# One kernel, two orders: the same attention and mixer operations of a Trainium2 core put into a new sequence

## The chip, the core and the metric

The kernel runs on one core of a Trainium2 chip. A core has five engines that run their own instruction streams side by side: TensorE (PE in the profile; its weight loads are shown apart, as PEld), VectorE (DVE), ScalarE (ACT), GpSimd (POOL) and SyncE (SP). They work on SBUF, the core's memory of 128 partitions, and on PSUM, eight banks into which PE writes. Each engine takes its instructions strictly in the order in which the program holds them; where one needs the result of another engine it waits on a semaphore, and everything behind it on its engine waits too. DMA transfers are issued from POOL and SP (and can be from ACT).

The metric is the time of one execution in microseconds. Three timed runs of the kernel before gave 284.23, 285.07 and 284.23 us; the median is 284.23.

## The reference

Eight sequences (B = 8) of 576 positions go through an attention of 8 heads of 64, and the result, 576 x 512 per sequence, through an MLP mixer:

```
attention:  scores = q k^T / 8, position i sees block j of 64 when i // 64 >= j // 64
            x = softmax(scores) v                    heads side by side: x is 576 x 512
token mix:  u = x + ( relu(x^T w_tok1) w_tok2 )^T    w_tok1 576 x 256, w_tok2 256 x 576
channels:   out = u + relu(u w_ch1) w_ch2            w_ch1 512 x 1536, w_ch2 1536 x 512
```

Inputs and output are float32; the matrix products run in bfloat16 with float32 sums.

## The kernel before, in words

The kernel is one Python function that first describes about 1,500 operations and then emits them. `P.add(engines, cost, emit, deps, ...)` appends an operation: the engines that may run it, what it depends on, which PSUM banks it takes and gives back, and the function that emits its instructions. Operations are numbered in the order of these calls. Nothing is scheduled while the kernel is built: `Plan.placed` reads the string `ORDER`, a list of words such as `627Tbd`. The number is the operation, the capital letter its engine (T for PE, A for ACT, D for DVE, P for POOL, S for SP) and the small letters are the PSUM banks that it takes (a to d are the banks `mm`, e to h the banks `late`, s and t two double banks `sc` that exist only during the first attention). The operations are emitted in the order of the words, so that the words of one engine are that engine's queue. The semaphores follow from what the operations read and write.

The stages, with the operations that the text speaks of:

- **Start.** DVE clears some tiles (`init_tiles`, L340); one of them, 9, zeroes the operand of the warming matmuls. `raise_clock` has PE run 11 matmuls of 512 columns on zeros (operation 43, L366) and then single extra ones (44 to 80, L373) wherever ORDER places them; their results are used by nobody.
- **Loads.** K and Q of a batch come in two groups of four heads. For the first group of batch 0, SP loads K in two halves (16, 13), ACT casts them to bfloat16 (17, 14; L395), and POOL loads Q in three pieces (21, 19, 23). All other loads of K, Q and V, and of the weights, are issued by POOL (L419, L471, L482, L505) and change the type on the way. DVE then transposes K and Q in blocks of 32 x 32 (L442).
- **Attention.** `score_set` (L569) multiplies 32 rows of K by Q for four heads at a time, which use the four 32-row strips of the PE array side by side, and adds a bar for the masked block. ACT takes the exponential (L587 and L737 in batch 0, L776 after it). The last 64 columns are copied and cleared by DVE or POOL (`tail`, L595 and L600). `head_out` (L617) and `ends_out` (L670, 64 columns of the array) multiply with V, whose extra column of ones gives the sum, and DVE divides (L637, L643, L692, L698).
- **Token mix.** `token_up` (L811, L815), then products with `w_tok2` (L910, in batch 0 L846), to which DVE adds x (L925): that is U. The channel products need U transposed. For batches 0 and 1 PE does it with the identity matrix (operation 12 makes it, on POOL); from batch 2 on SP does it with two DMA transposes per batch (L977), the first two of which are operations 607 and 606.
- **Channel mix.** Batch 0 plainly (`channel_up` L1038, `first_down` L1460). Batches 1 to 3 and the joined last 64 positions of all batches use Strassen-like sums of seven products (`channel_up_half` L1111, `channel_down_fast` L1369), batches 4 to 7 in pairs (`channel_up_fast` L1235). DVE and ACT keep, join and clip the parts (L395, L797, L1150, L1165, L1351), DVE adds the residual (L1393), and SP, at the end also ACT, stores the output (L1435).

Batches overlap: while PE does the channel products of one batch, it also does the attention of the next ones. ORDER is where that interleaving is written down. The line numbers are those of the profile of the kernel before; in the changed file the lines behind ORDER are one less.

Of the kernel before, what the change touches and what calls it, by code (L numbers as in the profile page):

```python
# [27 lines left out]
class Plan:  # L28
# [69 lines left out]
    16S 0A 11D 10D 13S 9D 21P 1D 2D 43Ta 5D 19P 4D 3D 23P 33P 27P 14A 25P 31P 15D 29P 17A 20D 37P 44Tb 45Tb 46Tb 22D  # L98
    47Ta 36P 48Ta 49Ta 18D 50Ta 51Ta 52Ta 35P 53Ta 24D 54Ta 55Ta 56Ta 125Ts 34P 100Ttbc 179P 126A 28D 57Ta 58Ta 59Ta
    176P 60Ta 61Ta 26D 62Ta 101A 12P 106Ts 63Ta 32D 182P 64Ta 107A 65Ta 104Tt 42P 30D 66Ta 67Ta 105A 68Ta 39P 123Ts  # L100
    102D 103D 69Ta 70Ta 41P 119A 71Ta 157Tt 124A 112Td 40P 113T 116Ta 108Tb 114D 120A 38P 109T 115D 138Ts 158A 181D
    81P 72Td 73Tc 74Tc 121D 75Tc 122D 139A 82P 76Tc 7D 144Tt 110D 111D 84P 135Td 178D 127Tc 145A 161Ts 185P 136D
    117D 137D 140D 131Tb 180D 83P 128T 162A 142Tt 177D 90P 132T 129D 143A 77Td 89P 163Ts 130D 133D 86P 134D 78Td
    164A 118D 141D 159D 200Tdcba 160D 85P 203A 173Te 154Tf 165Tg 202A 91P 174D 166T 155D 156D 201A 184D 92P 205Tbhfc
    204A 183D 169Td 88P 170T 209A 167D 263Ta 168D 208A 175D 150Tc 171D 261Tg 172D 207A 187D 267Td 206A 87P 186D
    146Te 262A 147T 264A 151T 268D 237Tgbfh 152D 339P 6D 148D 269Ta 153D 241A 149D 273Td 189P 240A 270D 281Tc 239A
    274D 265Te 190P 238A 271Ta 8D 282D 275Tb 266A 191P 193Tdhfg 276A 272D 283Te 196A 277Tc 342P 194A 315Ta 278D
    306Tb 197A 188P 294Td 195A 279Tc 284A 192P 318Tf 198D 280D 291Tg 319T 348P 316T 309Tc 317A 310T 257D 93P 320A
    307T 295T 94P 308A 292T 311A 258D 225Teahf 345P 296A 300Tb 227A 95P 285Tc 228A 286T 293D 226A 303Td 287D 229A
    304T 351P 232Tahge 341D 199D 312Tc 230D 233A 305D 313T 234A 231D 288Tf 344D 314A 297Ta 340D 236A 289T 343D 235A  # L110
    210Td 513P 245Tc 290A 211D 213Th 516P 212D 242Te 246D 216Tg 354P 247D 301T 214D 215D 248Td 243D 302A 298T 244D
    355P 217D 219Tc 249D 299A 250D 222Th 220D 254Te 221D 363Tdbaf 255D 256D 251Tc 349D 364A 330Te 352P 252D 365A
    218D 253D 321Td 367A 223D 224D 366A 259D 353P 368Tcghb 420Ta 372A 370A 422Tb 347D 371A 525P 346D 322T 421D 423A
    260D 369A 356Tafgh 323T 359A 357A 350D 424Tb 360A 324D 331T 358A 425D 388Tcadg 361P 514D 430Tb 391A 434Th 332T
    389A 431D 435A 518D 426Td 392A 517D 400Thcbf 390A 515D 428Tg 404A 393P 362D 334Ta 522P 403A 429D 677P 401A 335T
    333D 402A 528P 427D 376Tb 373Tc 394D 527P 96D 395Tdfgh 379Te 526P 377D 396A 374D 336T 375D 397A 519P 378D 380D
    405Tc 398A 680P 381D 382Tb 399A 406D 385Td 407D 432Te 337D 417Tc 383D 386D 433A 530Tafgh 387D 384D 418D 436Td
    419D 531A 440Tb 97D 414Tc 534A 325Te 533A 98D 326T 532A 415D 437A 416D 542Tahgf 99D 441A 438Tc 545A 327T 439D
    544A 444D 463Tgd 543A 445D 448Thb 328D 466A 464Tc 451D 546A 329S 411Ta 408Te 465A 446D 469T 412D 690P 413D 449Tf
    523D 470A 454T 529P 450A 409D 442Ta 410D 452Tc 455A 443D 691P 467Tg 520D 453A 537Taefh 447D 692P 468A 456T 521D  # L120
    538A 473T 689P 524D 539A 471T 679D 540A 683P 596Ta 457D 541A 474D 562Tcefh 597A 678D 458T 566A 681D 594Ta 565A
# [6 lines left out]
    694Tcgab 508D 856P 618T 698A 849D 509T 697A 846D 696A 619D 695A 760Tb 609D 610D 699P 510D 738Tacgh 761A 848D  # L128
    631Tf 742A 611D 942P 628Tb 741A 632D 758Th 700P 740A 853P 629D 739A 845D 635T 759A 726Tcbag 636D 723Th 730A 637T
    724D 729A 725D 717Tf 638D 762Th 727A 764Ta 728A 718D 719D 640T 763D 731P 733Tfcbg 641A 732P 765D 768Th 737A 851D  # L130
    766Td 772S 735A 720Ta 769D 711Tg 736A 746Tc 721D 722D 734A 616Th 767D 714Ta 617A 613Tb 712D 773S 713D 642Tdf
    747D 614A 748D 620T 715D 645A 716D 743Tg 622T 621D 639A 648T 744D 511S 745D 646Tb 854D 512S 649A 861Tcagh 338S
    647A 623D 643Td 863A 624D 652T 862A 644D 752Ta 865A 650T 653D 625T 864A 753D 749Tc 754D 626A 655T 866P 852D
    868Tadhg 867P 651D 656A 755Te 871A 770Tf 775D 952P 869A 654D 794Tbh 756D 750D 872A 751D 951P 795Ta 776D 797A
    779Tgc 757D 939P 796D 870A 780Te 782A 800T 657D 798Ta 781A 855D 783Td 771A 785T 799A 784D 948P 809Tef 801A 953P
    802T 777D 812A 778D 787T 803D 945P 786A 804T 815T 788D 789T 805D 816A 905Tbadg 790D 813Te 908A 807T 906A 814D
    792T 808A 810Td 658D 907A 817T 909A 811D 661Tbh 793A 818D 873Tadcg 662D 819T 875A 943D 667T 876A 820D 877A 944D
    874A 822T 941D 893Tdceg 821D 823A 887Ta 659D 897A 884Tf 663T 894A 888D 889D 895A 885D 886D 896A 940D 900Tadcg
    898P 664D 890Tf 904A 899P 881Te 949D 1037P 903A 925Tb 882D 955P 883D 902A 891D 892D 901A 878Te 947D 1040P
    968Tfcdg 926A 950D 954P 922Ta 969A 879D 665Tb 880D 1046P 971A 946D 970A 923D 924D 1043P 972A 956Tedfa 666D 913Tc  # L140
    668D 959A 916Tg 914D 669T 958A 915D 917D 957A 918D 660D 960A 910Td 919Tc 961D 995Tgafe 911D 1052P 920D 921D 670D
    999A 927Tc 1053P 998A 912D 962D 997A 791D 1050P 963Tdbef 996A 671T 928A 1042D 967A 1041D 966A 1000Tacgf 965A
    672D 979Te 964A 1039D 976Tb 1003A 673T 980D 977D 1004A 981D 978D 1002A 988Tbedg 1001A 674D 973Tc 991A 1047D
    1022Tf 676S 990A 974D 975D 989A 1038D 982Ta 992A 985Tc 806D 1054Tdbhe 983D 1023A 984D 993P 1020Tg 1044D 994P
    1055A 1051P 1048D 1058A 1045D 931Ta 1057A 1008Td 986D 1056A 987D 933Tf 932D 1021A 929Tc 1009D 934D 935Tb 1028Ta
    930D 1061Tehgf 1029D 937S 1032Tc 1062A 936D 1017Ta 1064A 1010D 1011Te 1063A 1018D 1014Td 1019D 1012D 1005Tb
    1033A 938S 1013D 1030Ta 1015D 1065A 1006D 1093Tecgh 1059D 1007D 1060P 1016D 1024Tf 1049P 1031D 1095A 1254Tb
    1094A 824D 1035S 1097A 1086Tdcae 1255D 1252Th 1090A 1025D 1089A 825D 828Tbe 1087A 1088A 826D 1253A 1091P
    1066Tadcf 1096A 829D 1092P 1026Th 1067A 830T 1070A 1027D 1069A 1034S 1068A 1098Tagfh 831D 834T 1099A 827D 1100A
    675S 1102A 1080Tc 774S 1074Td 1101A 1081D 1106Tb 835D 1112Ta 1071Tg 1107D 832Th 1108D 1113D 1082D 1114D 1072D  # L150
    1073D 1109Tb 1077Tc 1110D 1115Ta 1111D 1083Tg 1078D 1079D 1103Tb 1084D 838T 833D 1116D 1085D 1104D 1105D 1137Tfc
    1118D 836T 839D 1117D 1119D 1138Tb 840T 1120D 1139A 837D 1140A 1075D 1197Tba 842S 841D 1198Tg 1143T 1200D 843S
    1141Th 1076D 1036S 1144A 1258Te 1142D 1203T 1201Tf 1259D 1204A 1147T 1202D 1199A 1145T 1268Td 1148D 1121D
    1182Tbe 1146D 1269A 1207T 1185D 1205T 1183Td 1208D 1188T 1184D 1186Tg 1266Th 1206D 1187A 1150T 1267D 1190T 1151A
    1210T 1191D 1152Tdf 1211A 1272Tc 1155A 1192T 1273D 1189A 1278Ta 1193D 1156Tc 1279A 1158T 1209A 1157D 1153Tb
    1282S 1167Tah 1154D 1159A 1160T 1162T 1170A 1161D 1168Td 1171Tb 1163D 1122Tcg 1169D 1172A 1165T 1125D 1173T
    1166A 1260Td 1397D 1174A 1175T 1398D 1126Tf 1399D 1128T 1400D 1123Ta 1176D 1195T 1127D 1124A 1177T 1196A 1262Tb
    1178D 1129A 1256Ta 1132T 1263D 1270Tc 1133D 1180T 1130T 1271D 1181A 1135T 1261D 1416Tbc 1136A 1280S 1417Te 1194A
# [1425 lines left out]
```

## Time and profile before

| | |
|---|---|
| median of three runs | 284.23 us |
| profiled execution, its span | 284.7 us |
| PE busy | 275.8 us, 97% of the span |
| DVE busy | 240.3 us, 84% |
| ACT busy | 180.4 us, 63% |
| POOL busy | 71.7 us, 25% |
| instructions | 9438, of them 4038 matmuls and as many weight loads |

How to read it: the page lists the engines' busy time, a strip of 40 slices, the DMA queues, the chain of work that ended last, and the costliest groups of instructions as "line engine operation, out<-in". Matmuls are pipelined and overlap in the records, so that the time from one start to the next tells more than the duration of one. A row of the timeline gives start, length and what it is; in square brackets stands the idle time of that engine before it and what ended it. "issue" is idle time for which the profile shows no wait. A row of a DMA view gives the sender, the count, the size and the time from issue to landing.

### The profile page before, as it was taken

What the parts mean: (1) busy time and instruction counts of PE and PEld (TensorE: products, weight loads), DVE (VectorE), ACT (ScalarE), POOL (GpSimd) and SP (SyncE); (2) the same over time, 40 slices, a digit from 0 to 9 for tenths busy, and PEclk for the clock granted to TensorE, in tenths of its full rate; (3) what the DMA queues carried; (4) which work ended last, traced back from release to release, by engine and by line L of the source; (5) the groups of instructions that cost most, each with busy time, mean ns of one, the idle gap of its engine ahead of it and who ended that gap; (6) DMA issues with size and microseconds to landing.
All of it is one profiled execution on the core that took longest, in us unless ns stands there. A gap on an engine that the chain in (4) does not pass through costs nothing.

```text
span 284.7 us, 9438 instructions
## 1 busy us (share of the span) xinstructions
PE 275.8 (97%) x4038; PEld 197.6 (69%) x4038; DVE 240.3 (84%) x519; ACT 180.4 (63%) x325; POOL 71.7 (25%) x120
## 2 busy tenths in 40 slices
PE   7998999999999899999999999999999999999994
PEld 3667656556878676987777658744488876468883
DVE  3589569799999799999998997997998987598893
ACT  3798685778888358996879785136546653764000
POOL 8975635170641062060341220000000000000000
PEclk9999999999999999999999999999999999999999
DMA  8999999969989495898199587130033403000246
GB/s 160 166 174 202 190 205 203 137 94 134 144 120 119 71 84 87 225 135 122 11 169 102 87 106 132 49 119 18 2 74 98 126 7 131 12 2 0 104 127 212
DMA packets 64776, 31.79 MB, mean 112 GB/s; under 512 B 53088, under 2 KB 55904, under 8 KB 64736
## 3 DMA queue, kind: packets, MB, share of 16 engines
q0 software_dynamic: 45040, 17.64, 53.1%
q1 hardware_dynamic: 19696, 13.57, 19.6%
q8 instruction: 31, 0.51, 0.7%
q14 instruction: 9, 0.07, 0.1%
HBM read 35.85 MB, written 9.44 MB: 159 GB/s over the span
## 4 chain that ended last, share of the span: by engine, by line
PE 92%; DVE 2%; ACT 2%; DMA 1%; issue 1%; SPq 0%; DVEq 0%
PE late L1369 14%; PE mm L1369 11%; PE late L1235 7%; PE mm L1111 7%; PE late L1111 6%; PE mm L569 6%; PE mm L1235 6%; PE mm L617 4%; PE mm L811 3%; PE mm L910 3%; PE mm L1038 3%; PE late L569 2%; PE late L617 2%; PE late L811 2%; PE mm L1460 2%; PE late L1460 2%
## 5 line engine op out<-in xcount | busy, mean ns | idle before, releaser
L776 ACT ACTIVATE e_sb<-late 128x512 bf16<-128x512 f32 x89 | 50.5, 609 | 10.4 <-PE late L569 9.1
L776 ACT ACTIVATE e_sb<-mm 128x512 bf16<-128x512 f32 x79 | 45.1, 609 | 9.9 <-PE late L569 6.6
L471 POOL DMA_DIRECT2D vals<-in_v_dram x45 | 37.2, 844 | 26.7 <-PE late L617 15.9
L442 DVE STREAM_TRANSPOSE qk_sb<-qk_sb 128x288 int32<-128x288 int32 (+2 forms) x57 | 36.2, 694 | 4.6 <-ACT qk_sb L395 3.5
L1369 PEld LDWEIGHTS <-sums 128*128 128x128 bf16 x288 | 27.6, 98 | 5.6 <-issue 1.8
L1369 PEld LDWEIGHTS <-gT 128*128 128x128 bf16 x288 | 27.8, 98 | 4.6
L569 PEld LDWEIGHTS <-qk_sb 32*64 32x64 bf16 x1280 | 19.9, 104 | 13.1 <-issue 8.8
L569 PE MATMUL mm<-qk_sb 32*64 32x64 bf16 (+7 forms) x546 | 27.8, 291 | 0.0
L569 PE MATMUL late<-qk_sb 32*64 32x512 bf16 (+7 forms) x594 | 27.1, 291 | 0.0
L617 PEld LDWEIGHTS <-e_sb 128*128 128x128 bf16 x640 | 23.8, 97 | 4.1 <-issue 0.9
L1111 PEld LDWEIGHTS <-ws_sb 128*128 128x128 bf16 x192 | 17.8, 98 | 3.4 <-issue 1.3
L797 ACT ACTIVATE gT<-mm 128x512 bf16<-128x512 f32 x25 | 14.7, 601 | 7.8 <-PE mm L1111 3.0
L617 PE MATMUL mm<-vals,e_sb 128*128 128x65 bf16 x430 | 19.0, 193 | 0.0
L643 DVE TENSOR_TENSOR x_sb<-mm,rinv 128x256 bf16<-128x256 f32 x43 | 17.9, 421 | 1.1
L1111 PEld LDWEIGHTS <-wc_sb 128*128 128x128 bf16 x144 | 15.4, 114 | 1.8 <-issue 0.2
L1235 PEld LDWEIGHTS <-ws_sb 128*128 128x128 bf16 x96 | 9.3, 98 | 10.1 <-issue 0.2
L1369 PE MATMUL late<-wd_sb,sums 128*128 128x256 bf16 x108 | 13.6, 272 | 1.2 <-issue 1.2
L1369 PE MATMUL late<-wd_sb,gT 128*128 128x256 bf16 x120 | 14.7, 273 | 0.0
L595 POOL COPY vals<-e_sb 128x256 bf16<-128x256 bf16 x10 | 4.1, 412 | 40.9 <-issue 22.9
L395 ACT COPY mm<-late 128x512 f32<-128x512 f32 x17 | 9.9, 584 | 7.1 <-PE late L1235 5.0
L797 ACT ACTIVATE gT<-late 128x512 bf16<-128x512 f32 x17 | 10.2, 602 | 6.3 <-PE late L1235 3.4
L1235 PE MATMUL late<-e_sb,ws_sb 128*128 128x512 bf16 x44 | 12.6, 379 | 0.0
(203 smaller groups left out, 656.2 us busy)
## 6 DMA issues: line engine op xcount, KB each, us to landing
out_dram<-o_sb SPq DMA_DIRECT2D x14, 512.0 KB, 3.1
vals<-in_v_dram POOLq DMA_DIRECT2D x28, 128.0 KB, 5.4
qk_sb<-in_k_dram POOLq DMA_DIRECT2D x12, 288.0 KB, 6.3
qk_sb<-in_q_dram POOLq DMA_DIRECT2D x12, 288.0 KB, 5.9
out_dram<-o_sb SPq DMA_DIRECT2D x7, 256.0 KB, 3.2
wc_sb<-in_moe_w_ch_dram POOLq DMA_DIRECT2D x8, 192.0 KB, 7.7
wc_sb<-in_moe_w_ch_dram POOLq DMA_DIRECT2D x3, 512.0 KB, 10.4
vals<-in_v_dram POOLq DMA_DIRECT2D x15, 64.0 KB, 4.9
```

Of the source, the lines that this page charges most:

```text
L442: nc.vector.transpose(dst[:, 0:S, :] .rearrange("p s e -> p (s e)") .bitcast(I32) .rearrange("p (a k) -> p k a", k=NB)[:, k0:k1], raw2.bit ...
L471: nc.gpsimd.dma_start(out=t[128 - p : 128, J, hs, 0:64], in_=src)
L569: nc.tensor.matmul(out=home(n)[64 * half : 64 * half + 64, c : c + w], lhsT=bar[r, 0] if j is None else kT[i][r, 64 * j : 64 * j + 64, par ...
L617: nc.tensor.matmul(out=u[:, I, 0:65], lhsT=e[:, h, c : c + 128], rhs=vt[:, J, head, 0:65], start=(J == 0), stop=(J == I),)
L643: nc.vector.tensor_tensor(out=xt[:, 0:4, 64 * head : 64 * head + 64], in0=u[:, :, 0:64], in1=ri[:, 0:4].to_broadcast([128, 4, 64]), op=MULT,)
L776: nc.scalar.activation(dst, bank_of(x), EXP, scale=scale)
L797: nc.scalar.activation(dst, src, RELU)
L811: nc.tensor.matmul(out=ps, lhsT=w1_sb[:, c, tt : tt + 255 : 2], rhs=xt[:, c, cols], start=(c == 0), stop=False)
L1111: nc.tensor.matmul(out=bank_of(bank)[:, 256 * o_ : 256 * o_ + 256], lhsT=x(o_, m), rhs=y[:, :, m, :], start=opens, stop=m == 1, skip_group ...
L1235: nc.tensor.matmul(out=bank_of(bank), lhsT=x(m), rhs=y[:, :, m, :], start=first and m == 0, stop=m == 1, skip_group_check=not first,)
L1369: nc.tensor.matmul(out=bank_of(bank)[:, 256 * i : 256 * i + 256], lhsT=x[:, kk, 128 * i : 128 * i + 128], rhs=y[:, kk], start=first and i ...
L1460: nc.tensor.matmul(out=ps, lhsT=gT[0][:, cc, 128 * si : 128 * si + 128], rhs=wc2_sb[:, cc, :], start=cc == 0, stop=cc == NDC - 1,)
```

## The change

The words of ORDER are put into a new sequence. The operations and what each computes stay the same, with these exceptions: the extra warming matmuls (before, 35 of 256 columns; after, 23, of which 13 have 512 columns and 10 have 256), and the engine of 87 operations: 38 go from ACT to DVE, 36 from DVE to ACT, 11 change between DVE and POOL, and two stores of the output go from SP to ACT. The loads that POOL and SP issue at the start keep their order, up to the identity, which comes later. Some operations also take other PSUM banks.

The code that changes beside ORDER:

```diff
             bank = {"covers": False}
+            w = 512 if n % 4 else 256
 
-            def emit(o, bank=bank):
+            def emit(o, bank=bank, w=w):
                 nc.tensor.matmul(
-                    out=bank_of(bank)[:, 0:256], lhsT=zeros[:, 0:128], rhs=zeros[:, 0:256],
-                    start=True, stop=True,
+                    out=bank_of(bank)[:, 0:w], lhsT=zeros[:, 0:128], rhs=zeros[:, 0:w], start=True, stop=True,
                 )
 
             P.add(
-                "PE", 0.11, emit, pads["zeros"], 1e6, take=[(BANK, bank)], give=[bank], at=5.0 + 0.12 * n, until=20.0,
+                "PE", mm_cost(w, 1), emit, pads["zeros"], 1e6, take=[(BANK, bank)], give=[bank], at=3.0, until=20.0,
                 quick=True,
             )
```

The first words of ORDER, before and after:

```diff
-    16S 0A 11D 10D 13S 9D 21P 1D 2D 43Ta 5D 19P 4D 3D 23P 33P 27P 14A 25P 31P 15D 29P 17A 20D 37P 44Tb 45Tb 46Tb 22D
-    47Ta 36P 48Ta 49Ta 18D 50Ta 51Ta 52Ta 35P 53Ta 24D 54Ta 55Ta 56Ta 125Ts 34P 100Ttbc 179P 126A 28D 57Ta 58Ta 59Ta
+    5D 0A 21P 4D 2D 19P 11D 10D 23P 1D 33P 9D 27P 16S 17A 3D 18D 43Ta 50Tb 72Tb 44Tb 13S 14A 22D 25P 31P 29P 37P 20D
+    49Tb 15D 24D 26D 32D 51Tb 100Tsbc 101A 102D 104Tt 105A 45Td 55Td 56Td 36P 123Ts 124A 35P 61Td 34P 106Tt 57Td
```

The words around the token mix of batch 2 and its DMA transposes (607S, 606S), up to the first channel product that reads them (627T):

```diff
-    459D 564A 460D 476T 563A 595D 461T 477A 569Tchfe 682D 462A 472D 604Ta 847P 571A 478Tdb 475D 686P 572A 605D 602Tg
-    535P 481A 600Th 603D 536P 570A 598Ta 567P 482Tf 601D 607S 568P 553Tc 844P 599D 483A 479Tg 550Th 554D 555D 480A
-    488T 551D 484T 552D 606S 489D 486T 485A 556Tc 487D 491T 573A 574Thadg 557D 490D 492A 547Te 558D 577A 493D 497Tbf
-    575A 548D 576A 549D 559Tc 578A 688D 701Tedah 498A 685D 579Tg 560D 704A 684D 499T 705A 494D 850P 702A 693P 580D
-    585Ta 703A 581D 503T 500D 687D 706Tgdbh 586D 587D 561D 591Te 504D 710A 501Ta 709A 495D 708A 592D 707A 593D 582Tc
-    502D 627Tbd 612The 608D 630A 588Tg 583D 496D 505T 859P 615D 858P 633T 584D 506D 507T 857P 634A 589D 590D 860P
+    483A 475D 681D 569Tefbg 678D 572A 570A 488T 477D 691P 571A 602Ta 603D 486T 487D 573A 489D 484T 485A 574Tfeba
+    577A 567D 686P 604Tg 605D 550Tc 551D 552D 329S 598Th 553Tb 554D 576A 568P 599D 585Tg 586D 578A 607S 490A 588Ta
+    587D 556Tc 557D 491T 600Th 559Tg 589D 601D 606S 558D 575A 591Tf 592D 593D 560D 582Te 583D 590D 584D 561D 555D
+    547Th 548D 460A 549D 492A 497Tdc 498A 579Te 701Tgafb 703A 702A 499T 580D 581D 704A 690P 688D 706Tehga 710A 707A
+    847P 493D 705A 501Tf 693P 708A 500D 627Tea 494D 495D 496D 844P 502D 612Tbd 630A 503T 615A 608D 685D 618T 504D
...
```

More of the change, by code (lines that the diff above doesn't have):

```diff
@@ new lines @@
+    619A 857P 709A 684D 859P 633T 634A 505T 506D 687D 694Tgbhe 698A 846D 697A 609D 695A 610D 507T 758Th 696A 508D
+    738Tbgef 699D 700D 740A 759A 509T 510D 628Th 739A 629A 742A 741A 611D 717Tb 718D 719D 631Tg 632D 760Tc 849D
+    726Tbefh 637T 848D 638D 761A 730A 764Tc 765D 635T 636D 727A 766Tb 768Th 729A 769D 850P 640T 728A 767D 733Tgecf
+    641A 737A 853P 720Th 721D 722D 734A 735A 711Ta 712D 613Tb 614A 714Tf 845D 715D 773S 731P 732P 736A 743Th 744D
+    616Tg 713D 770Te 771A 723Ta 856P 716D 745D 617A 861Thfcb 863A 724D 855D 725D 762Te 864A 763D 772S 620T 642Tfa
@@ new lines @@
+    643Tc 622T 645A 621D 646Tg 865A 854D 948P 942P 862A 623D 512S 648T 649D 939P 752Tb 753D 866P 754D 746Th 747D
+    748D 647A 652T 625T 644A 626A 868Tcfeb 870A 755Th 749Td 951P 851D 954P 653D 756D 650T 871A 757D 869A 651D 872A
+    655T 775D 953P 809Teh 639D 750D 751D 656A 779Tcf 780Tb 794Tag 782A 781A 858P 795Td 654D 776D 797A 860P 796A 624D
+    785T 783Tb 800T 798Td 812A 815T 784A 777D 778D 867P 799A 786D 801A 787T 852D 788D 789T 790D 804T 511S 816A
+    905Taceb 909A 907A 906A 802T 805D 792T 793A 807T 908A 657D 808A 803D 810Tc 811D 661Tab 791D 873Tcefd 952P 658D
@@ new lines @@
+    1096A 1019D 1033D 1086Tacdg 1089A 1088A 1060P 931Th 1024Tf 1025D 1090A 1028Te 932D 824D 1087A 1254Tb 1066Tgfcd
+    1070A 1252Ta 1067A 1068A 1255D 1029D 1026Tb 1027D 1098Tegdh 1253A 937S 1074Tf 1091P 1092D 1069A 1075D 1101A
+    1071Tb 1072D 1076D 1102A 1080Tc 1034S 1081D 1082D 1099A 1077Ta 1078D 825D 1079D 1030Td 1031D 828Thf 1112Tc
+    1083Ta 1084D 1113D 1114D 1073D 1100A 1115Tg 1116D 1085D 826D 829A 834T 827D 1103Ta 1104D 835D 1035S 830T 832Tb
+    838T 1109Tc 831D 1105D 833D 839D 1137Tha 1106Td 1107D 1140D 1117D 1118D 1119D 1110D 1111D 840T 1143T 841D
@@ new lines @@
+    1197Teg 836T 1200A 1203T 1204A 1108D 1120D 1138Tc 1139D 1144D 1121D 1141Tf 1142D 1198Td 1199A 837D 1201Te 1266Tc
+    1202A 1167Tdh 1267A 1036S 1170D 1147T 1148D 1207T 1208D 842S 1182Tbc 1185A 1145T 1146D 1205T 1150T 1151A 1149D
+    1210T 1211D 1206D 1188T 1189A 1256Ta 1257D 1186Tf 1187D 1268Tb 1269D 1262Ta 1263D 1173T 1174A 1183Te 1184A
+    1152Tbg 843S 1168Td 1155A 1270Ta 1169D 1271D 1192T 1193D 1158T 1156Td 1157A 1190T 1191D 1159A 1278Ta 1279A
+    1153Te 1171Tf 1154A 1172A 1209A 1122Tab 1125D 1260Te 1261D 1160T 1162T 1163D 1177T 1161D 1175T 1176D 1282S
```

118 lines of the change are left out of this document (49 added, 69 removed).

## The prediction

> **What bounds the kernel now.** I read the page first, then the time windows, then the chain of waits in order of time, then the timeline of single engines where the chain leaves TensorE.
>
> ```profile
> span 284.7 us, 9438 instructions
> PE 92%; DVE 2%; ACT 2%; DMA 1%; issue 1%; SPq 0%; DVEq 0%
> ```
>
> ```profile
> 0.00:10.00 10.00, 7.80 (x82) 4.34 (x82) 4.58 (x15) 3.75 (x6) 8.54 (x18) 1.00 0.99 160
> 10.00:20.00 10.00, 10.00 (x214) 6.25 (x213) 7.07 (x25) 9.82 (x13) 8.72 (x16) 1.00 1.54 174
> 80.00:100.00 20.00, 18.76 (x324) 14.69 (x323) 18.32 (x42) 13.31 (x26) 4.38 (x10) 1.00 0.89 99
> ```
>
> The columns of the windows are length, then busy time of PE, weight loads, DVE, ACT and POOL. PE carries 92% of the chain. Between 10 and 20 us ACT is as full as PE: there the exponentials set the pace and the warming matmuls fill PE. In 80 to 100 us PE loses 1.24 us. A busy PE could still be one that waits inside its queue, so I look at the rate.
>
> ```profile
> 207.83 6.55 PE late L1369 x60
> 50.14 0.86 PE mm L811 x4
> 48.95 0.97 PE mm L811 x4
> 93.13 1.24 issue
> ```
>
> Sixty matmuls of 256 columns take 6.55 us, 0.109 us each, and four of 512 columns 0.86 us, 0.215 each: these are the fastest rates that the trace shows anywhere. Late in the kernel nothing stands between them, so a new order has nothing to win there. What it can win is the start, the pause of 1.24 us and the 0.11 us by which the run at 48.95 is longer than the one at 50.14; the longer one is followed by score matmuls on 32 rows of the array. It can lose wherever it brings a consumer too near to its producer.
>
> **The start.** All loads before the first scores keep their places; the memsets, casts and transposes behind them change.
>
> ```profile
> 1.33 0.27 DVE L340 MEMSET wd_sb<- 128x256 uint32 x1
> 2.05 0.33 DVE L340 MEMSET vals<- 128x32 bf16 x2 [0.16 <-issue]
> 1.66 4.66 PE L366 MATMUL mm<-wd_sb 128*128 128x512 bf16 x11 [1.66 <-DVE wd_sb L340]
> 6.16 1.58 PE L373 MATMUL mm<-wd_sb 128*128 128x256 bf16 x13
> 5.20 1.25 ACT L395 CAST qk_sb<-gT 128x576 bf16<-128x576 f32 x2 [2.95 <-DMA gT<-in_k_dram]
> 5.90 2.88 DVE L442 STREAM_TRANSPOSE qk_sb<-qk_sb 128x288 int32<-128x288 int32 x6 [3.51 <-ACT qk_sb L395]
> 8.29 0.42 PE L569 MATMUL sc<-qk_sb 32*64 32x512 bf16 x6 [0.54 <-DVE qk_sb L442]
> 8.98 3.84 ACT L587 ACTIVATE e_sb<-sc 128x1024 bf16<-128x1024 f32 x4 [2.54 <-PE sc L569]
> gT<-in_k_dram SPq DMA_DIRECT2D x1, 288.0 KB, 2.6
> gT<-in_k_dram SPq DMA_DIRECT2D x1, 288.0 KB, 4.0
> 1.25 1.76 POOL L437 DMA_DIRECT2D qk_sb<-in_q_dram  x3 [0.80 <-POOLq L1568]
> qk_sb<-in_q_dram POOLq DMA_DIRECT2D x1, 144.0 KB, 4.0
> ```
>
> Before, ACT casts the half of K that lands second first, and so both casts wait until 5.20. The new order casts the half that lands after 2.6 us first, and DVE transposes it first. Then the larger piece of Q sets the end: POOL issues three pieces from 1.25 on, this one second, near 1.9, and it lands 4.0 us later, near 5.9; with its own three transposes are left at 2.88/6 = 0.48 us each, so the first scores could begin near 7.5 instead of 8.29. But the memset of the zeros, which lets the warming start at 1.66, is third of eight now and seventh then: it ends near 2.4 (the seventh begins at 2.05). Eleven warming matmuls took 4.50 us up to 6.16, and five of the extra ones (three of 512, two of 256 columns: 3 x 0.215 + 2 x 0.109 = 0.86) stand ahead of the first scores: 2.4 + 4.5 + 0.86 = 7.8. That is a gain of 0.5. The first exponential came 0.69 behind the first score matmul (8.98 - 8.29); it follows a set of 44 matmuls instead of one of 8 now, for which I allow 0.15. I take **-0.35 us**, carried through the stretch that ACT fills. The bounds are 0 and -0.8.
>
> The 35 extra warming matmuls (35 x 0.109 = 3.8 us) become 13 x 0.215 + 10 x 0.109 = 3.9 us. I cost that at nothing: the ACT-bound stretch hides it. Without that cover it would be 0.1 us.
>
> **The identity and the channel weights.** POOL makes the identity later, and puts one clear of a score tail, which waits for an exponential of the first attention, ahead of seven of the eight loads of W1.
>
> ```profile
> 19.03 1.62 POOL L505 DMA_DIRECT2D wc_sb<-in_moe_w_ch_dram  x3
> 16.70 4.05 ACT L587 ACTIVATE e_sb<-sc 128x1024 bf16<-128x1024 f32 x4 [0.15 <-PE sc L569]
> ```
>
> POOL issued the first three from 19.03 on; behind a clear that stands next to the end of the exponentials (20.75) the second goes out about 2 us later than the 19.5 it had, and everything queued behind it on POOL too. The readers come behind the whole first U and two score sets, so I take 0, with 0 to +2 as bounds.
>
> **The tile shapes.** Changes into score matmuls, and into and out of the 64-column ends, cost the 0.11 us shown above. My count in ORDER is 70 of them before and 68 after: **-0.2 us**.
>
> **The crossbar transposes of batch 2: the place that decides.** `token_mix` adds U (601 is the last of four adds), SP then transposes it in two DMAs (607, 606), and the channel products read them, op 627 first.
>
> ```profile
> 83.85 0.67 DVE L925 TENSOR_TENSOR u_sb<-mm,x_sb 128x512 bf16<-128x512 f32 x1
> L977 SPq DMA_TRANSPOSE uT<-u_sb x2: 1351/2120/2890, 83.4 to 84.8; - x2
> DMA to landing us min/median/max: 10.0/10.3/10.6
> 81.37 1.08 POOL L419 DMA_DIRECT2D qk_sb<-in_q_dram  x2 [4.53 <-DVE qk_sb L442]
> qk_sb<-in_k_dram POOLq DMA_DIRECT2D x1, 288.0 KB, 10.1
> 94.37 0.60 PE L1369 MATMUL late<-wd_sb,sums 128*128 128x256 bf16 x4 [1.24 <-issue]
> 97.54 0.60 PE L1111 MATMUL mm<-uT,wc_sb 128*128 128x256 bf16 x4
> ...
> L977 SPq DMA_TRANSPOSE uT<-u_sb x2: 1232/1574/1916, 112.7 to 115.0; - x2
> DMA to landing us min/median/max: 3.0/3.3/3.5
> L977 SPq DMA_TRANSPOSE uT<-u_sb x1: 1329/1329/1329, 165.8 to 165.8; - x1
> DMA to landing us min/median/max: 5.1/5.1/5.1
> ```
>
> Beside three loads of Q and K (two of Q issued at 81.37, one of K that itself took 10.1 us) these two transposes took 10.0 and 10.6 us; the pair of batch 3, alone, took 3.0 and 3.5; one of batch 5, beside a load of V, 5.1. Before, none of it hurt: the second was issued at 84.8, its reader started at 97.54, 12.7 us later, and PE had 22 operations between the matmul that feeds the last add (598 there) and 627. In the new order ten stand between 600, which feeds the last add, and 627: three head outputs, two ends, three down products of 12 matmuls and two score sets. Their prices:
>
> ```profile
> 86.00 0.47 PE L617 MATMUL mm<-vals,e_sb 128*128 128x65 bf16 x10
> 86.30 0.60 PE L1111 MATMUL mm<-th_sb,wc_sb 128*128 128x256 bf16 x4
> 95.55 0.44 PE late L670 x20
> 161.39 0.58 PE late L569 x22
> 87.90 1.31 PE late L1369 x12
> ```
>
> 3 x 0.30 (86.00 to 86.30) + 2 x 0.44 + 3 x 1.31 + 2 x 0.58 + 2 x 0.11 for changes of shape = 7.1 us of PE work. The add takes 0.67 and the hand-overs about 0.15, so **6.3 us** are left for the transpose. What runs beside it? On POOL a V load, a Q load, a V load and a K load (690, 847, 693, 844) stand right behind the tail clear 568; the readers that their buffers wait for stand well ahead, so nothing holds them back, and 568 is next to 607 in ORDER. So again two loads of 288 KB run beside the transposes, with V loads in place of the third. I take 9.5 us, near the 10.0 of the same transfer and a little under it for the missing load: PE waits 9.5 - 6.3 = **+3.2 us** at 627. The ends are 0 (3.0, alone) and +4.3 (10.6). The pause at 93.13 lies in the same stretch, inside one of the down products that now stand ahead of 627, so a wait at 627 covers it: **-1.24 us**.
>
> The Trainium skill's page "DMA: Bandwidth & Descriptors", section "Queues, rings and completion order", says that each DMA engine takes turns between the queues, a packet at a time. By that rule a transpose beside loads should come through much as the one at 165.8 did; the 10.0 to 10.6 us speak against it here.
>
> Batch 3 gets a shorter gap too: behind the matmul that feeds its last add (762) stand ten channel products of four matmuls (4 x 0.109), three head outputs, an end and a score set, 4.4 + 0.9 + 0.44 + 0.58 + 0.2 = 6.5 us, less 0.8 for add and hand-overs: 5.7 us against 3.0 to 3.5 alone. Q and K loads stand close behind it on POOL; I take 0, with 0 to +4 as bounds if they collide as in batch 2. The rest of the order, where the 87 operations that change engine go about equally both ways between DVE and ACT, I take at 0 within 1 us: PE is the bound and both have slack (18 and 13 of 20 us in 80 to 100).
>
> **The tail.** The last output DMA moves from SP to ACT.
>
> ```profile
> 280.57 0.42 DVE L1393 TENSOR_TENSOR o_sb<-late,e_sb 128x256 f32<-128x256 f32 x1 [0.23 <-PE late L1369]
> ```
>
> The last fold of the new order is the same one, behind the same last matmuls, and its DMA still goes out as soon as it ends (280.99 here). No row shows a DMA issued by ACT; I take 0, within 0.3 to both sides.
>
> **Sum.** -0.35 - 0.2 - 1.24 + 3.2 = +1.4 us, so the profiled execution of 284.7 would become 286.1. The median of the runs, 284.23, is 0.5 below that execution; carried over it gives **285.6 us**, 0.5% slower. A measurement of this kernel can tell about 0.3% (0.85 us) from no change.
>
> **Rivals.**
> *The transposes come through in time.* At 5.1 us, the row beside the V load, 627 waits for nothing, the pause that came with the slow pair is gone too, and the time is 284.23 - 0.35 - 0.2 - 1.24 = **282.4**; with the pause kept 283.7. It decides below 6.3 us of landing. For it: only two loads of 288 KB run beside the pair now. Against: the K load that ran into the pair before is there again. That the engines take turns, as the Trainium skill's page has it, would make it so.
> *Both cancel.* A landing near 8 us costs 1.7, about what the start and the pause give: **284.2**.
> *The fast clock comes late.* The first eleven warming matmuls ran at 0.41 us, half the later rate. Their start moves by 0.7 us; if the clock rises only after the scores have begun, the five extra ones cost 0.8 more and the first score set 0.6 more: +1.4, **287.0** together with the wait at 627. Against it: the rate rose before 6.16, and the same eleven warming matmuls come first in the new order too. The Trainium skill, "TensorE: Matmul & The Clock Gate", Part 1, has the clock released by a free-running window of some 3.4 us; no run here shows its phase.
>
> **How the numbers follow.** Forecast (landing 9 to 10.6 us, 285.1 to 286.7): 0.44. Late clock on top: 0.08. Cancel: 0.14. In time: 0.34. So faster 0.34, same 0.14, slower 0.52. The range takes in the rival in time, 282.4, and goes up to the forecast with the late clock and a little of the bounds at the weights and at batch 3: 287.5. My own range for the forecast alone is 285.0 to 286.8.
>
> **What would show it.** Right: op 627, L1110 with uT as operand, waits some 3 us behind 501, the transposes of batch 2 land 9 us or more after issue, the first exponential starts near 8.6, and PE has no idle time after 200. Wrong: those land within 6 us; or PE stops at the channel weights before 36 us or at the first products of batch 3; or matmuls at half rate stand beyond 8 us.

## The result, and the profile after

The changed kernel takes **288.45 us** (median of 12 runs, 285.29 to 292.1); the kernel before takes 284.5 (12 runs, 283.8 to 286.19). The compared runs give a ratio of **1.0107, 95% interval 1.0075 to 1.0139**; the three slowest runs are not in that comparison, so the medians are further apart than the ratio says (1.4%). Predicted was 285.6, within 282.4 to 287.5: the sign is right, but the time lies outside that range.

From the page come the span and the chain that ended last, by engine; from the list of waits, what TensorE waited for (total, times, longest).

```profile
span 287.9 us, 9409 instructions
PE 92%; DMA 3%; DVE 2%; issue 1%; ACT 1%; DVEq 0%
```

```profile
PE mm L1110 <- DMA uT<-u_sb: 3.5, 1, 3.5
PE mm L365 <- DVE wd_sb L339: 2.1, 1, 2.1
PE late L568 <- ACT e_sb L586: 0.2, 1, 0.2
PE mm L1110 <- DVE x_sb L642: 0.2, 1, 0.2
```

DMA went from 1% to 3% of the chain. One wait is new: 3.5 us at the channel products that read `uT`, the place the prediction names. Of the others only the last, 0.2 us at 128.72, lies behind it. No other wait on the list is for a transfer, so here neither the channel weights nor the transposes of batch 3 hold TensorE up. Next the DMA view of the two crossbar transposes, and their piece of the chain in order of time.

```profile
L976 SPq DMA_TRANSPOSE uT<-u_sb x2: 1366/1369/1372, 85.7 to 88.5; - x2
DMA to landing us min/median/max: 7.0/8.4/9.8
```

```profile
87.83 0.69 DVE u_sb L924
88.52 0.03 DVE x_sb L642
88.54 9.75 DMA uT<-u_sb
```

The second transpose goes out at 88.54, right behind the last add, and lands 9.75 us later. The timeline of TensorE around it (start, length, matmuls, in brackets the wait):

```profile
93.38 1.48 PE L1368 MATMUL late<-wd_sb,sums 128*128 128x256 bf16 x12
98.34 1.06 PE L1110 MATMUL mm<-uT,wc_sb 128*128 128x256 bf16 x8 [3.48 <-DMA uT<-u_sb]
99.24 2.39 PE L1368 MATMUL mm<-wd_sb,sums 128*128 128x256 bf16 x12
101.43 1.06 PE L1110 MATMUL mm<-uT,wc_sb 128*128 128x256 bf16 x4
102.28 0.97 PE L1110 MATMUL late<-uT,wc_sb 128*128 128x256 bf16 x4
103.09 1.47 PE L1368 MATMUL late<-wc_sb,sums 128*128 128x256 bf16 x12
```

The work ahead of the reader ends at 93.38 + 1.48 = 94.86, which is 6.3 us behind 88.54. Then comes something the prediction does not have. From start to start, the eight matmuls behind the wait take 0.90 us, 0.11 each, but the four at 101.43 take 0.85 us, 0.21 each, and so do the next four; at 103.09 the rate is back. The windows (length, busy time of PE, weight loads, DVE, ACT, POOL, then the granted clock, the share of its full clock that TensorE was given) say why:

```profile
90.00:95.00 5.00, 4.87 (x88) 3.47 (x85) 4.90 (x12) 3.63 (x8) 1.77 (x2) 1.00 1.33 158
95.00:100.00 5.00, 1.66 (x14) 1.50 (x15) 3.04 (x5) 1.52 (x4) 0.00 (x0) 0.96 1.44 73
100.00:105.00 5.00, 5.00 (x72) 3.72 (x70) 1.72 (x3) 1.69 (x4) 0.56 (x1) 0.70 0.07 8
105.00:110.00 5.00, 5.00 (x71) 3.45 (x57) 3.17 (x9) 3.64 (x7) 0.54 (x1) 1.00 0.67 113
```

The granted clock is 1.00 up to the wait, 0.70 in the five microseconds after it, and 1.00 again. What is missing from full speed is 5 x 0.30 + 5 x 0.04 = **1.7 us**. So the wait costs twice: 3.5 us in which TensorE stands, and 1.7 us in which it then runs at half rate. The 12 runs fall into two groups by this: five with a mean clock of .998 or more took 285.29 to 286.98, seven with .994 or less took 287.85 to 292.1. The profiled one is of the second group.

### The profile page after: what moved, and what is told of

It is laid out like the page before. It is cut to its first block, busy times and chain, and to the rows that moved or that the text cites. A ratio compares the mean times of both kernels' runs of the same rounds, so it can differ in the third digit from the quotient of the medians.

```text
span 287.9 us, 9409 instructions
## 1 busy us (share of the span) xinstructions
PE 278.5 (97%) x4026; PEld 197.4 (69%) x4026; DVE 240.7 (84%) x520; ACT 176.8 (61%) x323; POOL 72.4 (25%) x121
## 4 chain that ended last, share of the span: by engine, by line
PE 92%; DMA 3%; DVE 2%; issue 1%; ACT 1%; DVEq 0%
PE mm L1368 14%; PE late L1368 10%; PE late L1234 7%; PE mm L1110 7%; PE mm L1234 5%; PE late L568 5%; PE late L1110 5%; PE mm L616 4%; DMA uT<-u_sb 3%; PE mm L810 3%; PE mm L1459 3%; PE mm L568 3%; PE mm L909 2%; PE late L616 2%; PE late L909 2%; PE late L1037 2%
## 5 line engine op out<-in xcount | busy, mean ns | idle before, releaser
L775 ACT ACTIVATE e_sb<-late 128x512 bf16<-128x512 f32 x99 | 55.8, 611 | 5.9 <-PE late L568 4.7
L775 ACT ACTIVATE e_sb<-mm 128x512 bf16<-128x512 f32 x69 | 41.0, 615 | 11.3 <-PE late L568 5.7
L568 PE MATMUL late<-qk_sb 32*64 32x64 bf16 (+7 forms) x668 | 27.3, 289 | 0.2 <-ACT e_sb L586 0.2
L568 PE MATMUL mm<-qk_sb 32*64 32x512 bf16 (+7 forms) x472 | 27.2, 293 | 0.0
L394 ACT COPY late<-late 128x512 f32<-128x512 f32 x15 | 8.7, 585 | 14.4 <-PE late L1234 12.4
L394 ACT COPY mm<-late 128x512 f32<-128x512 f32 x11 | 6.3, 575 | 14.0 <-PE late L1110 4.3
L1368 PE MATMUL mm<-wd_sb,sums 128*128 128x256 bf16 x102 | 13.5, 285 | 0.0
L1392 DVE TENSOR_TENSOR o_sb<-mm,u_sb 128x512 f32<-128x512 f32 x15 | 10.2, 683 | 4.0 <-PE mm L1368 4.0
L586 ACT ACTIVATE e_sb<-sc 128x1024 bf16<-128x1024 f32 x11 | 10.7, 1028 | 4.4 <-PE sc L568 4.2
L418 POOL DMA_DIRECT2D qk_sb<-in_k_dram x12 | 6.7, 558 | 24.0 <-DVE qk_sb L441 18.2
```

What stands on the lines that cost most here:

```text
L394: nc.scalar.copy(dst, src)
L568: nc.tensor.matmul(out=home(n)[64 * half : 64 * half + 64, c : c + w], lhsT=bar[r, 0] if j is None else kT[i][r, 64 * j : 64 * j + 64, par ...
L775: nc.scalar.activation(dst, bank_of(x), EXP, scale=scale)
L1368: nc.tensor.matmul(out=bank_of(bank)[:, 256 * i : 256 * i + 256], lhsT=x[:, kk, 128 * i : 128 * i + 128], rhs=y[:, kk], start=first and i ...
```

## The experiments

**Theory A**: everything the change costs is the wait at 627, made by loads that run beside the transposes, and the fall of the clock that follows the wait. **Rival B**: other parts of the new order cost it too. **Rival C**: the transposes are slow for a reason other than the loads. **Rival D**: the clock falls for a reason other than the wait. Ratios are to the kernel before, run in turns on the same chip.

### The loads out of the way

Early, the four loads that POOL issued from 85.5 on go out as soon as their buffers are free:

```diff
+    690P 693P 847P 844P
     568P
...
-    690P
...
-    847P
...
-    693P
...
-    844P
```

> The changed kernel with the four loads 690, 693 (V) and 847, 844 (Q, K) ahead of the clear 568 in POOL's queue, so that they go out from about 78 us on and not from 85.5 on; nothing else is moved. Theory A (the loss is the wait for the crossbar transposes at 627, and the fall of the granted clock that follows from it): the second transpose, issued near 88.5, runs nearly alone and lands in 3 to 5 us, 627 waits less than 0.5 us, the granted clock stays at 1.00 throughout, and the time falls by 3.5 + 1.6 from 288.45 to about 283.3, up to 284.5 if the instruction pause of the old order comes back. Rival B (the rest of the new order costs it: start, engines exchanged, weight loads): 286.5 or more, with the wait gone.

Late, the same four words stand behind `857P`, which waits until 91.6:

> The changed kernel with the same four loads behind the V load 857, which waits for products of batch 2 until about 91.7 us: the transposes run with no load beside them. Theory A: both land in 3.0 to 3.5 us like the pair of batch 3 before, 627 does not wait, clock 1.00; 283.3 to 285.5, the upper end if the scores of batch 3 then wait for Q and K. Rival B: 286.5 or more. Rival C (the transposes are slow for another reason than the loads beside them): still 7 us or more to landing, and about 288.4.

And only Q and K early (`847P 844P` ahead of `568P`), or only V early (`690P 693P` ahead of `568P`):

> The changed kernel with only the Q and the K load (847, 844) ahead of 568; the V loads 690 and 693 stay beside the transposes. If a V load costs a transpose little, as at 165.8 in the kernel before (5.1 us), the second one lands within 6.3 us, 627 does not wait, and the time is 283.3 to 284.5. If any load beside it makes it slow, the wait is 2 to 3.5 us and the time 286 to 288.4.

> The changed kernel with only the V loads 690 and 693 ahead of the clear 568; the Q and the K load (847, 844) go out right behind it, from 85.5 on, beside the transposes. With only V beside them the transposes took 3.6 and 5.7 us. If Q and K are what slows them, the second one takes 7 us or more and 627 waits 1 to 3 us: 285.5 to 287.5. If the number of bytes is what counts, it takes 4 to 6 us, 627 does not wait, and the time is about 284.5.

The DMA view of the transposes, in this order: four loads early, four late, Q and K early (V beside), V early (Q and K beside):

```profile
L976 SPq DMA_TRANSPOSE uT<-u_sb x2: 1232/1292/1351, 85.8 to 88.6; - x2
DMA to landing us min/median/max: 3.1/3.9/4.7
```

```profile
DMA to landing us min/median/max: 3.0/3.5/3.9
```

```profile
DMA to landing us min/median/max: 3.6/4.7/5.7
```

```profile
DMA to landing us min/median/max: 7.4/8.3/9.2
```

| loads beside the transposes | landing, us | wait at 627 | median, us | ratio |
|---|---|---|---|---|
| V, Q, V, K (the change) | 7.0 and 9.8 | 3.5 | 288.45 | 1.0107 (1.0075 to 1.0139) |
| none issued beside them, four early | 3.1 and 4.7 | none | 284.51 | 0.9972 (0.995 to 0.9995) |
| none issued beside them, four late | 3.0 and 3.9 | none | 284.8 | 0.9995 (0.9972 to 1.0017) |
| V, V | 3.6 and 5.7 | none | 284.56 | 0.9971 (0.9951 to 0.9991) |
| Q, K | 7.4 and 9.2 | 1.2 | 285.45 | 1.0032 (1.0009 to 1.0054) |

Four words of POOL's queue take the whole loss away; the mean clock is then .998 or more in every run of these four. B and C fall. The early loads are not all done when the transposes go out: in the run with four early, Q and K are issued at 81.08 and 81.62 and land 6.7 and 8.1 us later, K near 89.7, and yet the transposes issued at 85.8 and 88.6 take only 3.1 and 4.7 us. With the same V loads early but Q and K issued at 85.24 and 85.78 they took 7.4 and 9.2 us. So Q and K make the transposes late when they are issued close to them; a K load that was merely still moving did not. By their ratios the three without a wait stand at 283.7 to 284.4 where before stands at 284.5; I had expected 283.3 of A. What the rest of the new order is worth is taken up in the last group.

### Bytes or kind of load

Three more V loads (689, 692, 691) beside the transposes, seven in all:

> The changed kernel with three more V loads (689, 692, 691), which go out at 74 to 77 us there, behind the clear 568 and ahead of 690, so that POOL issues seven loads beside the transposes: V from 85.5 on, Q near 89, K near 90.5. If a transpose gets through only as the loads beside it leave room, the second one takes 10 us or more, 627 waits 4 us or more, the granted clock falls in all runs, and the time is 289 or more. If Q and K alone make it slow, it meets them later and takes 6 to 9 us: a wait of 0.5 to 3 us and 285 to 287.5, with a clock of 1.00.

Second, Q and K early and all five V loads beside:

> The changed kernel with Q and K (847, 844) ahead of the clear 568, and all five V loads (689, 692, 691, 690, 693; 4 x 128 + 64 = 576 KB, as much as Q and K have together) behind it, from 85.5 on. If the bytes beside a transpose slow it, the second one takes 8 to 9.5 us as beside Q and K, and 627 waits 1.5 to 3 us: 286 to 288.8. If it is the kind of load, V being milder than Q and K, the second one takes about 5.7 us as beside two V loads, 627 waits for nothing, and the time is about 284.6.

The wait and the DMA view of the first, then of the second:

```profile
PE mm L1110 <- DMA uT<-u_sb: 4.4, 1, 4.4
```

```profile
DMA to landing us min/median/max: 5.9/8.3/10.7
```

```profile
PE mm L1110 <- DMA uT<-u_sb: 1.1, 1, 1.1
```

```profile
DMA to landing us min/median/max: 5.8/6.6/7.4
```

With seven loads the wait is 4.4 us, both runs have a clock of .994 or less, and the time is 291.06 (ratio 1.0221, 1.0174 to 1.0268). With 576 KB of V the slower transpose takes 7.4 us, between the 5.7 beside 192 KB of V and the 9.2 beside 576 KB of Q and K: 285.8 us, 1.0035 (1.0013 to 1.0056). So with more V issued beside it the transpose came later, and with Q and K later than with as many bytes of V. Each of these is one profile, and five profiles of the changed kernel spread from 8.5 to 9.8 us, so the sizes are rough. POOL issued the V loads over 4.2 us and the two others within 1.1 us, so that part of the difference may be their density; this stays open.

### The clock

The loads stay, and warming matmuls fill the wait; 12 words for the full fill, 4 for the part, each with one more matmul that the banks ask for:

```diff
+    62Te 63Te 65Te 66Te
...
     627Tea
```

> The changed kernel with 12 more of its warming matmuls of 512 columns ahead of 627, and one more that the order of the banks asks for: 13 x 0.215 = 2.8 us of idle work inside the wait of 3.5 us. The loads stay. Theory A, second half (the granted clock falls because PE stood still for 3.5 us): the wait that is left is under 1 us, no matmul at 0.18 to 0.21 us stands behind 627, the granted clock is 1.00, and the time is 288.45 - 1.6 = 286.9, with all runs within about 1 us of each other. Rival D (the clock falls for another reason, such as the load on the chip): 288.4 and a clock of .993 in most runs, as in the changed kernel.

> The changed kernel with 4 more warming matmuls of 512 columns ahead of 627 and the one more that the order of the banks asks for: 5 x 0.215 = 1.08 us of idle work in the wait, so that PE stands still for 1.5 to 2.5 us and not for 2.5 to 3.5. If the clock falls only where PE stands still for longer than some 3 us, all runs have 1.00 and the time is that of the full fill, 286.9, as the wait ends when the transpose lands. If 2 us are enough, a part of the runs still shows .994 or less and the median is 287.5 to 288.4.

TensorE's timeline with the full fill (its lines are one higher, like those of the kernel before; one of the twelve matmuls is missing from the records):

```profile
94.61 2.75 PE L374 MATMUL late<-wd_sb 128*128 128x512 bf16 x11
97.42 1.04 PE L1111 MATMUL mm<-uT,wc_sb 128*128 128x256 bf16 x8
98.29 1.47 PE L1369 MATMUL mm<-wd_sb,sums 128*128 128x256 bf16 x12
```

The transposes are as late as ever (6.1 and 8.6 us), the useful work begins at 97.42, but the twelve matmuls at 98.29 now run at 0.11 us each. All eight runs lie between 286.77 and 287.61, median 286.89, ratio 1.0057 (1.0034 to 1.0079), as A had it. With the part fill 1.3 us of wait are left, all four runs have .999 or more and 285.98 to 287.24, median 286.93 (1.0068, 1.0043 to 1.0093). None of these 12 runs has a fall, with the loads in place and the transposes late; so it is the idle time that makes the clock fall, and rival D is out. The part fill was meant to leave 1.5 to 2.5 us and left less, so it does not say how long the idle time must be. For that, the changed kernel once more, timed, and three more profiles of it:

> The changed kernel once more, on the same chip as the others. Theory A: runs of two kinds, some with a granted clock of 1.00 and 285.3 to 287.0 us and some with .994 or less and 287.8 to 292; median 1.0 to 1.5% over before. In the profile the wait at 627 is 2.5 to 4 us; where the clock is at 1.00 in it, the matmuls behind the wait run at 0.109 us each and not at 0.18 to 0.21.

> One more profile of the changed kernel, to set the length of the wait at 627 against the clock. So far a wait of 3.5 us came with a fall (span 287.9, clock .993) and one of 2.4 us without (285.1, 1.00). If the length decides, a wait under 2.5 us has 1.00 and a span of 282.7 plus the wait, and one over 3.5 us has a fall and 1.5 us more.

> The changed kernel again, for one more pair of wait and clock. Waits of 2.44 and 2.50 us came without and with a fall. If the fall hangs on where the wait lies against a period of the clock and not on its length alone, waits between 2 and 3 us go on to come with either, and a fall is again a stretch of 3.4 us at half rate, 1.7 us of loss.

> The same once more: with a fall the span is 282.4 to 283.4 plus the wait plus 1.7 us, without one it is 282.4 to 283.4 plus the wait.

The timelines behind the wait, of the first and of the second of these:

```profile
97.20 1.06 PE L1110 MATMUL mm<-uT,wc_sb 128*128 128x256 bf16 x8 [2.44 <-DMA uT<-u_sb]
98.10 1.47 PE L1368 MATMUL mm<-wd_sb,sums 128*128 128x256 bf16 x12
99.41 0.60 PE L1110 MATMUL mm<-uT,wc_sb 128*128 128x256 bf16 x4
```

```profile
97.46 1.49 PE L1110 MATMUL mm<-uT,wc_sb 128*128 128x256 bf16 x8 [2.50 <-DMA uT<-u_sb]
98.75 2.75 PE L1368 MATMUL mm<-wd_sb,sums 128*128 128x256 bf16 x12
101.31 0.63 PE L1110 MATMUL mm<-uT,wc_sb 128*128 128x256 bf16 x4
```

After 2.44 us the twelve matmuls take 1.31 us from start to start, after 2.50 us they take 2.56.

The trace also holds the granted clock as a list of stretches. In the profile after, the full clock begins at 7.46 us and lasts 92.16 us; then come 3.413 us at half, up to 103.04, and the full clock again. The half stretch is 3.413 us long in all five profiles with a fall, and in all 17 profiles each stretch at full clock is a whole number of times as long (92.16 is 27 x 3.413). So the clock changes only at edges that lie 3.413 us apart, and the start of the full clock gives their place in each profile. The table sets against them the idle time at 627, split where an edge cuts it:

| wait at 627, us | idle time, by window | clock 95 to 100, 100 to 105 | span, us | span less wait |
|---|---|---|---|---|
| 4.42 (seven loads) | 1.23 and 3.19 | 0.97, 0.69 | 289.0 | 284.6 |
| 3.48 (the change) | 1.35 and 2.13 | 0.96, 0.70 | 287.9 | 284.4 |
| 2.50 (the change) | 2.50 | 0.79, 0.86 | 287.0 | 284.5 |
| 2.48 (the change) | 2.48 | 0.73, 0.92 | 286.8 | 284.3 |
| 2.44 (the change) | 1.15 and 1.29 | 1.00, 1.00 | 285.1 | 282.7 |
| 2.25 (the change) | 2.21 and 0.04 | 0.70, 0.96 | 286.5 | 284.2 |
| 1.2 (Q and K beside) | 1.03 and 0.14 | 1.00, 1.00 | 283.6 | 282.4 |
| 1.1 (576 KB of V beside) | 1.13 | 1.00, 1.00 | 283.9 | 282.8 |

With a fall the rest is 284.2 to 284.6, without one 282.4 to 282.8: a fall costs 1.4 to 2.2 us, and the missing clock of each row (5 us times what lacks to 1.00 in both windows) is 1.7 to 1.75, half of 3.413 us. The length alone does not decide, since 2.25 had a fall and 2.44 had none. What sorts the rows is the idle time inside one window: with 2.13 us or more the clock falls at the edge that ends that window, with 1.35 or less it does not. For the row of 3.48 that edge is at 99.62, 1.3 us after TensorE has started again; the wait of 2.44 was cut in two by an edge at 95.91.

The timed runs of the second look at the change say the same as the first: two of five kept the clock (286.19, 286.88), three did not (287.98 to 292.41); median 287.98, ratio 1.0094 (1.0052 to 1.0136).

### What the rest of the order is worth

The kernel before once more, for a second profile of it:

> The kernel before once more, for a second profile of it. The changed kernel's times are its spans plus 1.8 us (287.9 and 289.68, 283.5 and 285.29); by that the profiled execution of before, span 284.7, took 286.5 and not some half a microsecond more than the median of 284.23, which is a span of 282.4. Theory P (the two stalls of that profile for which no wait is shown, 1.24 us at 93.13 and 0.75 us at 27.68, are an accident of that execution): a profile whose span is near 282.5 shows neither, or under 0.4 us together, so that covering them can save a median run nothing. Rival Q (they belong to the order): at least the one at 93.13 is there again with over 0.8 us, and the span is 283.7 or more.

Its span, its whole list of TensorE's waits, a window, and ACT's timeline:

```profile
span 282.9 us, 9438 instructions
```

```profile
PE mm L366 <- DVE wd_sb L340: 1.7, 1, 1.7
PE mm L811 <- DVE x_sb L643: 0.3, 1, 0.3
PE mm L569 <- DVE x_sb L643: 0.2, 1, 0.2
```

```profile
90.00:95.00 5.00, 5.00 (x84) 3.98 (x81) 4.91 (x12) 3.19 (x7) 1.23 (x2) 1.00 1.09 113
```

```profile
4.32 1.25 ACT L395 CAST qk_sb<-gT 128x576 bf16<-128x576 f32 x2 [2.07 <-DMA gT<-in_k_dram]
8.53 3.84 ACT L587 ACTIVATE e_sb<-sc 128x1024 bf16<-128x1024 f32 x4 [2.96 <-PE sc L569]
```

This execution took 284.66 us, 1.8 above its span, and shows no pause at 93 and none at 27 (no wait on its list is put down to "issue"); theory P holds in this profile. The profile of the first part, span 284.7, was thus one of 286.5 us, slower than each of the 12 runs of before (of 29 further runs of it, three took 286.4 or more). Its pauses belong to that execution, and so does its late K: here the casts begin at 4.32 and not at 5.20, and the first exponential at 8.53, earlier than the changed kernel's 8.83. The changed kernel's start, TensorE and then ACT:

```profile
2.06 4.88 PE L365 MATMUL mm<-wd_sb 128*128 128x512 bf16 x11 [2.06 <-DVE wd_sb L339]
6.73 1.40 PE L373 MATMUL mm<-wd_sb 128*128 128x512 bf16 x5
8.05 0.33 PE L568 MATMUL sc<-qk_sb 32*64 32x320 bf16 x2
8.83 3.77 ACT L586 ACTIVATE e_sb<-sc 128x1024 bf16<-128x1024 f32 x4 [4.01 <-PE sc L568]
```

From start to start the eleven warming matmuls take 4.67 us, 0.42 each, and the five behind them 1.32, where 0.86 was forecast: by the list of stretches the full clock begins only at 7.46 here. (The windows show 1.00 from the start on; that half rate can be read only from the matmuls and from where the list begins.) Two more runs put the rest to the test: the early loads with the clear of the zeros first (`9D` ahead of `5D`), and the early loads again with more rounds.

> The kernel with the four loads early (they go out from 78 us on), and beside that the clear of the zeros, 9, first of DVE's clears. If the start is worth what the prediction said (0.35 us, carried through the stretch of the exponentials), the warming begins near 1.3 instead of 2.06, the extra matmuls are done by 7.3, the first scores follow the Q transposes near 7.8, the first exponential comes at 8.5 to 8.6 instead of 8.77, the last of that stretch ends at 20.5 instead of 20.7, and the time is 284.2 to 284.4. If another thing sets the stretch, its end stays at 20.7 or 20.8 and the time at 284.5.

> The kernel with the four loads early once more, with more rounds, for the question whether the new order without its collision beats the old one. The first time it stood at 0.9972 of before (0.995 to 0.9995). If the rest of the new order is worth what the prediction said beside the wait (0.35 for the start, 0.2 for the shapes), the ratio is 0.998 or less with an interval below 1; if these are worth nothing it is 0.999 to 1.001.

ACT's timeline in the stretch of the exponentials, the early loads as they were, and with the zeros first:

```profile
8.77 3.77 ACT L586 ACTIVATE e_sb<-sc 128x1024 bf16<-128x1024 f32 x4 [3.75 <-PE sc L568]
19.70 1.02 ACT L586 ACTIVATE e_sb<-sc 128x1024 bf16<-128x1024 f32 x1 [0.20 <-PE sc L568]
```

```profile
8.59 3.77 ACT L586 ACTIVATE e_sb<-sc 128x1024 bf16<-128x1024 f32 x4 [3.62 <-PE sc L568]
19.61 1.03 ACT L586 ACTIVATE e_sb<-sc 128x1024 bf16<-128x1024 f32 x1 [0.21 <-PE sc L568]
```

The first exponential comes 0.18 us earlier, the last 0.09, and the time stays: 284.57 us, ratio 0.9995 (0.9982 to 1.0008). The warming matmuls are done early there, and TensorE waits 1.4 us for the transposes of Q instead. The early loads again give 284.48, 0.9992 (0.9973 to 1.001). The old kernel against itself, in the run above, came out at 0.9985 (0.9973 to 0.9998), so a tenth or two of a per cent is nothing here. The five results without a wait lie between 0.9971 and 0.9995: the best version found is as fast as the kernel before, or faster by some 0.3%.

## Why the prediction was wrong, step by step

- **The wait at 627: right, place, cause and about the size.** The 6.3 us left for the transpose are the 88.54 to 94.86 of the profile. The landing taken, 9.5 us, was measured at 9.8, 8.7, 8.8, 8.5 and 8.8 in five profiles of the changed kernel, the wait of +3.2 at 3.5, 2.4, 2.5, 2.25 and 2.5. (The 10.0 and 10.6 it was taken from were 8.2 and 8.9 in the second profile of before.) That V, Q and K loads do it is shown by moving them. The Trainium skill, "DMA: Bandwidth & Descriptors", section "Queues, rings and completion order", has the engines take turns between queues, packet by packet. Its reading as "comes through in time" was the rival at 282.4; beside two V loads it did come through (5.7), beside Q and K it did not (9.2).
- **The clock behind the wait: missing, and the largest error.** The sum prices the wait by its length alone and has no term for what TensorE does when it starts again. A fall costs 1.7 us, and 13 of the 20 executions of this kernel on record have a mean clock of .994 or less; in two of them (.986 and .987; 292.1 and 292.41 us) about twice as much clock is missing, and no profile shows where. The prediction did name the fall-back of the rate as a sign of being wrong ("matmuls at half rate stand beyond 8 us"), but it looked for it only at the start, as "the fast clock comes late". The Trainium skill, "TensorE: Matmul & The Clock Gate", which it cited there, also states in Part 1 that the clock falls back after an idle window of some 3.4 us: 3.2 us of forecast wait lie just short of that, and the step left out was to make a fall behind 627 a rival of its own. The traces here show that less is enough: 2.13 us of idle time in one window of 3.413.
- **"-1.24 us", the pause at 93.13 that a wait at 627 covers: wrong.** The pause was in one execution; the median run of the old kernel has none to be covered. Underneath lies "the median of the runs, 284.23, is 0.5 below that execution": that sets a time beside a span. By the 1.8 us that lie between span and time in all later runs, the execution was 2.3 us above the median, and no stall found in it alone should have been carried to the median.
- **The start, -0.35 us: not there.** In 14 profiles with the new start (the run with the zeros first left out) the first exponential comes at 8.24 to 8.86, in the middle at 8.78, and only three of them before the 8.6 of the forecast; with the old start it came at 8.98 and, with a punctual K, at 8.53. Two things set it. Where the full clock begins late, as at 7.46 in the profile after, the five extra matmuls run partly at half rate and hold TensorE until 8.05, while the last Q transpose had ended at 7.78. Where it begins early (at 4.84 to 5.78 in three others of the changed kernel), TensorE waits 0.5 to 1.1 us for the Q transposes. Nor was a gain carried on: of the 2.25 and 2.48 us waits, the second had its first exponential 0.43 us earlier (8.24 against 8.67), and the span less wait is the same (284.2 and 284.3). With the zeros first, 0.18 us at the first exponential became 0.09 at the last one and nothing in the time.
- **The tile shapes, -0.2 us: open.** Start and shapes together would be 0.55 us, a ratio of 0.9981; the results without a wait lie on both sides of it, and the old kernel against itself is no further from 1 than that. No run changed the shapes alone.
- **At nothing, and right as far as the waits show:** the identity and the channel weights, batch 3 and the output DMA on ACT. None of them has a wait in the list of the profile after; with Q and K early one for the channel weights, 0.4 us, appeared. The change of the warming matmuls, also put at nothing, was not tried alone.

The sum, put together afterwards by what was measured: 284.5 + 2.5 for the wait (the middle of five) + 1.7 for the clock = 288.7, against 288.45. Set against the forecast of 285.6, the clock adds 1.7, the pause that was not there to cover 1.24, start and shapes at most 0.55 and the slower base 0.3, while the shorter wait takes 0.7 off: 3.1, where 2.85 were missing. Of the rivals, "in time" and "both cancel" needed a landing of 8 us or less; the late clock at the start came only in part: in the profile after, the rate rose at 7.46, behind the first of the extra matmuls and ahead of the scores.

## What to carry to other kernels

Price a new wait of TensorE by its length and, if it can put some 2 us into one of the clock's windows, by the slow clock behind it as well; a stall that cannot be avoided cost less here when idle matmuls filled it (286.9 against 288.45 us). Before a stall of one profile goes into a sum, set that execution's own time beside the median: a pause for which no wait is shown may not be there in the next one. When an order brings a reader nearer to a DMA, look at what the other queues send in the same microseconds: here four words of the POOL queue were the whole difference.

## What the runs showed of the hardware that I had not expected

- **A wait of 2.25 us was enough for the clock to fall, and one of 2.44 was not.** The clock changes at edges 3.413 us apart, whose place differs from one execution to the next, and the idle time inside one window decides: 2.13, 2.21, 2.48, 2.50 and 3.19 us each brought a fall of one window, 3.413 us at half rate; the longest without one is 1.38 us (the wait for Q in the run with the zeros first). The Trainium skill, "TensorE: Matmul & The Clock Gate", Part 1, describes a free-running window of about 3.4 us; the stretches agree with that. Its rule of thumb in "HAM oscillation — how this bites in real kernels", no idle gaps over some 3.4 us, is too mild here: 2.25 us was enough. The rule is read off profiles in which the wait fell against the edges by chance; no run here places a wait on purpose, and where between 1.38 and 2.13 us the limit lies stays open.
- **Crossbar transposes are delayed by loads of another queue that change the type, if these are issued beside them:** the slower of the pair took 3.9 us with none, 5.7 beside 192 KB of V, 7.4 beside 576 KB of V, 9.2 beside 576 KB of Q and K and 10.7 beside seven loads, one profile each.
- **An identical kernel differs from one execution to the next by the arrival of its first load:** K could be cast at 5.20 in one profile of the old kernel and at 4.32 in the other, and the first exponential moved from 8.98 to 8.53 with it.
